# Attention with a routed FFN on one core: the first batch's second chunk takes its two reused pairs late, the FFN's weights load two chunks later, and the FFN stands back behind the routing

## The chip, the cores and the metric

One Trainium2 chip, of which the program uses one core. The metric is device microseconds for one execution, from the first to the last instruction with what lies around them; less is better.

## The reference

For each of 8 batches of 3136 tokens: attention without a softmax, whose output gates `u`, and then a small FFN for the 128 tokens of the batch that score highest.

```python
def _attn_ref(u, v, z):            # u, v: (8, 3136, 256)   z: (8, 3136, 64)
    scores = (1.0 / S) * np.matmul(z, z.transpose(0, 2, 1))
    attn = np.maximum(scores, 0.0) ** 2
    return u * np.matmul(attn, v)

def _moe_ref(x, w_gate, w1, w2, capacity):      # w1: (256, 1024)   w2: (1024, 256)   capacity 128
    scores = np.einsum('bsd,d->bs', x, w_gate)
    out = x.copy()
    for b in range(B):
        top_idx = np.argpartition(-scores[b], capacity)[:capacity]
        xe = x[b, top_idx]
        ye = np.maximum(xe @ w1, 0.0) @ w2
        g = 1.0 / (1.0 + np.exp(-scores[b, top_idx]))
        out[b, top_idx] = xe + g[:, None] * ye
    return out

reference = lambda u, v, z, ...: _moe_ref(_attn_ref(u, v, z), w_gate, w1, w2, capacity)
```

## The kernel before

**Chunks and slots.** Each batch is cut into 7 chunks of output tokens: five of 512 (called c0 to c4 here), then one of 256 (c5) and one of 320 (c6). Each chunk runs over the batch's 24 groups of 128 tokens in pairs, and over a last half group by itself, so a chunk has 13 slots, s0 to s12, and a batch 91. The slots of all batches stand in one list, `slots`, and one loop goes through it; its index is `k`, and `SLOTS` is 13. In a slot, `mix` issues the pair's 12 matmuls into the accumulators `acc` (8 with the high part `hi` of the squared scores, 4 with the low part `lo`; the half group has 4). While the slot runs, `more_scores` prepares the pair that is used three slots later.

**New and old pairs.** A new pair needs four matmuls `sc<-Z,ZH` and `sc<-Z,ZL`, and after them relu, square and the split into `hi` and `lo` on ScalarE, VectorE and GpSimd. The matrix of scores is symmetric. So the five chunks of 512 also transpose what later chunks need (tile `aT`, of which there are two), SyncE stores it to DRAM (`squares`, `squares_narrow`, `squares_own`), and the later chunk fetches it into `qk` (three buffers) instead of computing it: an old pair. An old pair costs TensorE 12 matmuls instead of 16. A fetch is issued seven slots ahead of its first use (`AHEAD`), or later if the three `qk` buffers are taken. In c1 the old pairs are (0, 1) and (2, 3); each chunk spreads its old pairs evenly among the new ones.

**What else stands in the slots.** `plan` is a table from a slot's number to functions: loads for the next batch, fetches, and for the first batch the FFN's weights. `weight_tasks` loads each of eight pieces of `w1` and `w2` through the staging tile `vst`, splits it on ScalarE and GpSimd into `w_here` (the two tiles `wh` and `wl`, 1 MB each) and `keep_weight` stores the split halves to DRAM (`w1h_there` and so on), since only one of the two matrices fits.

**The queue of small tasks.** When a batch's last slot has been issued, `route` puts a list of tasks in the queue `far`, and they are worked off during the next batch's slots, one at a time. A task is a list of matmuls to mix into a slot's own, then functions for the other engines, and, if it has a third entry, the number of slots until the next one may start (two without it). When a chunk ends, `finish` queues two tasks of its own, which go ahead of these at s2 and s5 of the next chunk. In order, a batch's routed part is:

- `fold`, then eight times `total`: a search for the 128th highest score, three slots apart;
- `ahead` (then `quotas` and `spans` on VectorE) and `take`, which find the chosen tokens;
- `bring_weight(1)`, by which SyncE loads the split `w1` into `wh` and `wl`, and `number`; `gather`; an empty task; `weigh`; `turn`;
- the FFN: `hidden` for the first 512 columns (6 matmuls of 512), `turn_h` (4 transposes), `hidden` for the others, `bring_weight(2)`, which puts `w2` in `wh` and `wl` in place of `w1`, `turn_h`, and last `back`: 24 matmuls of 256 columns into `y`, with `scatter` behind them.

In `back` the first four matmuls use `wh`, the fifth is the first that uses `wl`. Batches 0 to 4 (counted from 0) go through the whole list, each during the batch after it. Batches 5 and 6 (`put_off`) leave the FFN for the end, and the last batch has a scheme of its own.

**Queues.** Every engine takes its instructions in the order in which they were issued. SyncE issues nearly all transfers in one row, and each waits there until its buffer is free. `ps_m` is one PSUM bank that the small tasks use one after the other.

Of the kernel before, what the change touches and what calls it, by code (L numbers as in the profile page):

```python
# [85 lines left out]
def attention_then_routed_ffn(ctx: ExitStack, tc: tile.TileContext, zt, ut, v, wg, w1, w2, cst, cst16, keys, outs, at, cap):  # L86
# [16 lines left out]
    SLOTS = NJ // 2 + 1  # L103
# [75 lines left out]
    def keep_weight(i):  # L179
        for here, there in zip(w_here, w_there[i - 1]):  # L180
            nc.sync.dma_start(there.bitcast(F32), here.bitcast(F32))
# [126 lines left out]
    for b in range(B):  # L308
        for c in range(NCH):
            old = [(2 * g, 2 * g + 1) for g in range(min(c, WHOLE) * GT // 2)]  # L310
            new = [(2 * g, 2 * g + 1) for g in range(min(c, WHOLE) * GT // 2, NJ // 2)]
            if c < WHOLE and (b or c):

                new.insert(len(new) - 2, new.pop(1))
            both = [((i + 0.5) / len(old), 0, js, True) for i, js in enumerate(old)]
            both += [((i + 0.5) / len(new), 1, js, False) for i, js in enumerate(new)]
            slots += [(b, c, js, is_old) for _, _, js, is_old in sorted(both)]
            slots.append((b, c, (NJ,), False))
# [28 lines left out]
    def spend(act=0.0, dve=0.0, pool=0.0):  # L347
        busy["act"] += act
        busy["dve"] += dve
        busy["pool"] += pool  # L350
# [187 lines left out]
    def put_off(b):  # L538
        return B - 1 - HELD <= b < B - 1 and merged(B - 1) > 0

    def merged(b):
        return LATE if b == B - 1 and 0 < cap <= P else 0
# [121 lines left out]
    def route(b):  # L664
# [59 lines left out]
        def settle(rd):  # L724
            junk = moe.tile([TP, NS], F32, name="enough", tag="enough")[:R]
            m = moe.tile([TP, 1], F32, name="m", tag="m")[:R]
            nc.vector.tensor_scalar(
                junk, st["ps"][:R, :NS], float(cap), None, op0=ALU.is_ge, op1=ALU.add, accum_out=m
            )
            mi = moe.tile([TP, 1], I32, name="mi", tag="mi")[:R]  # L730
            nc.vector.tensor_copy(mi, m)
            base = moe.tile([TP, 1], I32, name="base", tag="base", bufs=2)[:R]
            if rd == last:
                base = st["ps"][:R, 64:65].bitcast(I32)
            if rd == 0:
                k = moe.tile([TP, 1], I32, name="place", tag="place")[:R]
                nc.vector.tensor_scalar(
                    k, mi, 32 - BITS, INT_MIN, op0=ALU.logical_shift_left, op1=ALU.bitwise_xor
                )
                flip = moe.tile([TP, 1], I32, name="flip", tag="flip")[:R]  # L740
                nc.vector.tensor_scalar(
                    flip, k, 31, 0x7FFFFFFF, op0=ALU.arith_shift_right, op1=ALU.bitwise_and
                )
                nc.vector.tensor_tensor(base, k, flip, op=ALU.bitwise_xor)
            else:
                nc.vector.tensor_scalar(
                    base, mi, 32 - BITS * (rd + 1), st["base"], op0=ALU.logical_shift_left, op1=ALU.bitwise_xor
                )
            st["base"] = base
            spend(dve=0.6)  # L750
# [69 lines left out]
        def spans(r0):  # L820

            rank = consts["rank"][:R, r0 : r0 + P]
            taken, begin, end = st["taken"], st["begin"], st["end"]
            if r0:
                nc.vector.tensor_scalar(taken[:, NT : NT + 1], begin, -float(r0), -2.0 * NT, op0=ALU.add, op1=ALU.max)
                nc.vector.tensor_scalar_min(taken[:, NT : NT + 1], taken[:, NT : NT + 1], 2.0 * P)
            else:
                nc.vector.tensor_scalar_min(taken[:, NT : NT + 1], begin, 2.0 * P)
            upper = moe.tile([TP, P], F32, name="upper", tag="upper")[:R]
            nc.vector.tensor_scalar(upper, rank, end, None, op0=ALU.is_le)  # L830
            of = moe.tile([TP, P], BF16, name="of", tag="big", bufs=2)[:R]
            nc.vector.scalar_tensor_tensor(of, rank, begin, upper, op0=ALU.is_gt, op1=ALU.mult)
            st["of"] = of
            spend(dve=0.6)
# [6 lines left out]
        tasks = [([fold], [start, count], 3)]  # L841
# [4 lines left out]
        if late:  # L846
            tasks.append(([total], [lambda: settle(last), masks]))
            tasks += [([columns], keep_columns), ([places], ranks)]
            tasks += choose(st, 0, cap)
            choice[b] = st  # L850
        else:
            tasks.append(([total], [lambda: settle(last), masks, run_up]))
            tasks.append(([ahead], [quotas, lambda: spans(0)]))
            for r0 in range(0, cap, P):
                n = min(P, cap - r0)
                first, *ffn = expert(b, st, n, r0)
                if put_off(b) and b == B - 2:
                    tasks = [(*t[:2], 2) for t in tasks]
                if r0:
                    tasks.append(([], lambda r0=r0: spans(r0)))  # L860
                tasks.append(([take], None))
                tasks += first
                if put_off(b):
                    held.append(ffn)
                else:
                    tasks += ffn[0] + ffn[1]
# [13 lines left out]
    def choose(st, r0, n):  # L880

        R, NT = st["G"].shape
        QT = Q // 4
        NP = NT // QT

        def pick(q):
            oh = moe.tile([TP, QT, P], BF16, name="oh", tag="big", bufs=2)[:R]
            t = slice(q * QT, (q + 1) * QT)
            nc.vector.tensor_tensor(
                oh,  # L890
                consts["rank"][:R, r0 : r0 + P].rearrange("p (o r) -> p o r", o=1).broadcast_to([R, QT, P]),
                st["rk"][:, t].rearrange("p (t o) -> p t o", o=1).broadcast_to([R, QT, P]),
                op=ALU.is_equal,
            )
            st["oh", q] = oh
            spend(dve=1.1)

        def find(q):
            if q == 0:
                st["ps"] = misc_bank("ids")  # L900
            what = st["what"]
            for i in range(QT):
                t = q * QT + i
                nc.tensor.matmul(
                    st["ps"][:, : what.shape[2]], st["oh", q][:, i, :], what[:, t, :],
                    start=(t == 0), stop=(t == NT - 1),
                )

        def begin():
            tok = consts["tok_half16"][:R].rearrange("p (t w) -> p t w", w=2)  # L910
            what = moe.tile([TP, NT, 5], BF16, name="what", tag="what")[:R]
            nc.vector.tensor_copy(what[:, :, :2], tok)
            cut(st["G"], what[:, :, 2:])
            st["what"] = what
            pick(0)

        tasks = [([], begin), ([], lambda: pick(1))]
        for q in range(NP):
            then = (lambda q=q: pick(q + 2)) if q + 2 < NP else None
            tasks.append(([lambda q=q: find(q)], then))  # L920
        tasks[-1] = (tasks[-1][0], lambda: keep_choice(st))
        return tasks
# [256 lines left out]
    def at_slot(k, fn, act=0.0, dve=0.0):  # L1179
        if k < len(slots):  # L1180
            plan.setdefault(max(k, 0), []).append((fn, act, dve))

    def at_slots(k, load, use, act, dve=0.0, lead=2):

        at_slot(k, use, act, dve)
        loads.append((k - lead, load))
# [3 lines left out]
    for b in range(B):  # L1190
        k0 = b * per

        for i in range(NCH):
            if b == 0:
                k = (0, 0, 0, 1, 3, 5, 6)[i]
            elif i < WHOLE:
                k = k0 - per + (i + 1) * SLOTS + 7
            else:
                k = k0 - 1 + 4 * (i - WHOLE)
# [9 lines left out]
        for g in range(NJ // 2 + 1):  # L1209
            k = k0 - 10 + 3 * g // 2 if b else max(1, g - 2)  # L1210
# [20 lines left out]
    for (b, c, g), ks in used.items():  # L1231
        k = max(ks[0] - AHEAD, room.popleft() - LEAD + 2)
# [4 lines left out]
            at_slot(k - LEAD - 3, lambda key=(b, c): fetch_own(*key))  # L1237

    for i, (load, use) in enumerate(weight_tasks):
        k = (1 + i // 4) * SLOTS  # L1240
        loads.append((k + (8, 9, 11, 13)[i % 4], load))
        at_slot(k + 10 + i % 4 * 2, use, 0.6)
    for i in (1, 2):
        at_slot(i * SLOTS + 17, lambda i=i: keep_weight(i))
    at_slots(SLOTS + 1, load_consts, use_consts, 0.0, 0.7)
    for k, load in loads:
        at_slot(k, load)
# [83 lines left out]
    for k, (b, c, js, is_old) in enumerate(slots):  # L1331
# [5 lines left out]
        tasks = []  # L1337
# [126 lines left out]
```

## Time and profile before

| | |
|---|---|
| runs | median 2114.52 us of 3 (2112.32, 2114.52, 2115.31) |
| profiled execution | 2112.72 us; span 2110.9 us from the first to the last instruction, so 1.8 us lie around it |
| granted TensorE clock | 1.00 throughout |
| busy share of the span | TensorE 99%, weight load 83%, VectorE 74%, GpSimd 62%, ScalarE 60% |
| DMA | 412 MB, 195 GB/s on average; SyncE's queue is busy 70% of 16 engines' span |

The busy share counts a matmul from its start to a modelled end, and consecutive ones overlap, so 99% does not say that TensorE runs at its best; it does say that little idle time is left. Rows of the timeline read: start, length, engine (with a q where it is the issue of a transfer), line, operation, tiles, shape, count, and in brackets the idle time before it and what ended that.

### The profile page before, as it was taken

Reading aid. Unit: us, or ns where it says so; the run is one execution under the profiler, and the core shown is the slowest. Engines: PE = TensorE matmul, PEld = TensorE weight load, DVE = VectorE, ACT = ScalarE, POOL = GpSimd, SP = SyncE. Lnnn points to the kernel's source line nnn. Section 1 sums busy time; section 2 is a strip of 40 time slices with the busy share of each in tenths; the row PEclk is TensorE's granted clock in tenths of the full one; section 3 lists DMA queues with packets and bytes.
Section 4 is the critical chain, followed back from the end, with each engine's and each line's share of the span. In section 5 each row is a group of like instructions: output and inputs, shape, how many; then the busy total and the mean of one; then the engine's idle time right before and its main releaser. Section 6 shows DMA issues by size and latency. Waiting matters only on the chain.

```text
span 2110.9 us, 31339 instructions
## 1 busy us (share of the span) xinstructions
PE 2081.4 (99%) x10359; PEld 1750.4 (83%) x10359; DVE 1559.2 (74%) x2361; ACT 1263.3 (60%) x1570; POOL 1313.5 (62%) x703
## 2 busy tenths in 40 slices
PE   8999999999999999999999999999999999999999
PEld 6788978889888898888888888888888888887788
DVE  8766678775877668776678767787577876788776
ACT  7665576554766457654576546765467654775543
POOL 6676577645766458664587646766467655666643
PEclk9999999999999999999999999999999999999999
DMA  6698766787668766688666876678766776666862
GB/s 189 202 261 222 198 184 173 217 199 213 181 186 218 202 195 190 188 220 220 177 190 187 229 211 173 190 195 217 210 182 185 196 193 171 203 188 162 220 173 96
DMA packets 425730, 412.01 MB, mean 195 GB/s; under 512 B 147616, under 2 KB 338912, under 8 KB 421984
## 3 DMA queue, kind: packets, MB, share of 16 engines
q1 hardware_dynamic: 424512, 407.66, 69.8%
q0 software_dynamic: 768, 2.10, 0.3%
q8 instruction: 81, 1.33, 0.3%
q14 instruction: 81, 0.66, 0.1%
q10 hardware_dynamic: 288, 0.26, 0.0%
HBM read 235.31 MB, written 172.23 MB: 193 GB/s over the span
## 4 chain that ended last, share of the span: by engine, by line
PE 74%; DVE 6%; DMA 6%; ACT 5%; POOL 3%; issue 3%; SPq 2%; POOLq 0%; ACTq 0%; DVEq 0%
PE acc L521 60%; PE sc L415 12%; DVE a L436 2%; POOL lo L485 2%; ACT a L425 2%; ACT hi L426 2%; DMA vst<-in_v 2%; DMA qk<-squares_narrow 1%; DVE aT L454 1%; DMA wl<-w2l_there 1%; DVE lo L485 1%; DMA squares_narrow<-aT 1%; PE h L1104 1%; PE y L1148 1%; SPq L265 0%
## 5 line engine op out<-in xcount | busy, mean ns | idle before, releaser
L521 PE MATMUL acc<-hi,V 128*128 128x512 f32 (+2 forms) x5376 | 1226.0, 366 | 9.0 <-ACT hi L393 4.7
L485 POOL TENSOR_TENSOR lo<-a,hi 128x1024 fp32r<-128x1024 f32 (+2 forms) x327 | 740.8, 2268 | 609.3 <-DVE a L436 438.9
L521 PEld LDWEIGHTS acc<-hi,V 128*128 128x128 f32 x5376 | 930.3, 188 | 175.9 <-DVE ut L566 9.1
L521 PE MATMUL acc<-lo,V 128*128 128x512 f32 (+2 forms) x2688 | 664.2, 364 | 7.2 <-POOL lo L485 3.5
L425 ACT ACTIVATE a<-sc 128x1024 f32<-128x1024 f32 (+4 forms) x408 | 363.2, 890 | 493.2 <-PE sc L415 374.9
L521 PEld LDWEIGHTS acc<-lo,V 128*128 128x128 f32 x2688 | 471.4, 188 | 89.0 <-DVE lo L485 6.4
L436 DVE TENSOR_TENSOR a<-sc,a 128x1024 f32<-128x1024 f32 (+3 forms) x335 | 339.9, 1015 | 258.1 <-ACT hi L426 227.9
L393 ACT CAST hi<-qk 128x1024 fp32r<-128x1024 f32 (+2 forms) x320 | 274.4, 862 | 254.5 <-PE acc L521 204.5
L485 DVE TENSOR_TENSOR lo<-qk,hi 128x1024 fp32r<-128x1024 f32 (+2 forms) x230 | 348.2, 1523 | 84.4 <-ACT hi L393 83.2
L454 DVE STREAM_TRANSPOSE aT<-a 128x512 f32<-128x512 f32 (+1 forms) x520 | 341.0, 691 | 89.5 <-ACT a L431 62.7
L426 ACT ACTIVATE hi<-a 128x1024 fp32r<-128x1024 f32 (+4 forms) x408 | 377.4, 925 | 21.4 <-PE acc L521 5.0
L415 PE MATMUL sc<-Z,ZH 128*128 128x512 f32 (+2 forms) x760 | 280.8, 373 | 3.7 <-DVE a L436 2.1
L415 PE MATMUL sc<-Z,ZL 128*128 128x512 f32 (+2 forms) x760 | 278.2, 370 | 0.7 <-DVE ZL L121 0.7
L485 POOL TENSOR_TENSOR lo<-qk,hi 128x512 fp32r<-128x512 f32 (+2 forms) x90 | 172.9, 1924 | 61.1 <-issue 45.5
L415 PEld LDWEIGHTS sc<-Z,ZH 128*128 128x128 f32 x760 | 142.6, 188 | 35.0 <-DVE a L436 7.7
L415 PEld LDWEIGHTS sc<-Z,ZL 128*128 128x128 f32 x760 | 142.6, 188 | 25.3 <-DVE ZL L121 1.1
L121 POOL TENSOR_TENSOR V<-vst,V 128x512 fp32r<-128x512 f32 x89 | 128.2, 1445 | 28.5 <-ACT V L120 22.4
L587 POOL TENSOR_TENSOR ut<-x,w_run 128x1024 f32<-128x1024 f32 (+2 forms) x52 | 124.3, 2390 | 26.5 <-DVE x L578 25.7
L121 POOL TENSOR_TENSOR ZL<-zst,ZH 128x512 fp32r<-128x512 f32 (+2 forms) x56 | 69.4, 1244 | 17.1 <-ACT ZH L120 17.1
L431 ACT ACTIVATE a<-a 128x1024 f32<-128x1024 f32 x73 | 77.5, 1062 | 2.3
L120 ACT CAST V<-vst 128x512 fp32r<-128x512 f32 x95 | 57.7, 608 | 30.0 <-DMA vst<-in_v 30.0
L566 DVE SCALAR_TENSOR_TENSOR ut<-acc,ut 128x512 f32<-128x512 f32 (+2 forms) x112 | 64.1, 613 | 12.6 <-PE acc L521 12.4
(173 smaller groups left out, 1054.6 us busy)
## 6 DMA issues: line engine op xcount, KB each, us to landing
squares<-aT SPq DMA_DIRECT2D x160, 512.0 KB
qk<-squares SPq DMA_DIRECT2D x320, 256.0 KB
squares_narrow<-aT SPq DMA_DIRECT2D x320, 128.0 KB
qk<-squares_narrow SPq DMA_DIRECT2D x80, 512.0 KB
vst<-in_v SPq DMA_DIRECT2D x190, 128.0 KB
out<-x SPq DMA_DIRECT2D x162, 128.0 KB
ut<-in_ut SPq DMA_DIRECT2D x40, 512.0 KB
squares_own<-aT SPq DMA_DIRECT2D x39, 256.0 KB
```

What stands on the lines that cost most here:

```text
L121: (lo_on or nc.vector.tensor_tensor)(lo, src, hi.bitcast(F32), op=ALU.subtract)
L393: nc.scalar.copy(by(hi), src)
L415: nc.tensor.matmul(ps[:, q], z[:, j * P : (j + 1) * P], mov, start=z is ZH, stop=z is ZL)
L425: nc.scalar.activation(a, ps[:, :n], AF.Relu)
L426: nc.scalar.activation(pieces[0][0](hi), pieces[0][1], AF.Square)
L431: nc.scalar.activation(a, a, AF.Square)
L436: square = lambda: nc.vector.tensor_tensor(a[rows], ps[rows, :n], a[rows], op=ALU.mult)
L454: nc.vector.transpose(to, a[rows, q].rearrange("p (m t a) -> p m t a", t=GT, a=Q))
L485: on.tensor_tensor(view(lo), src, view(hi).bitcast(F32), op=ALU.subtract)
L521: nc.tensor.matmul(ac[h], w, mov, start=first and h not in started, stop=stop)
L566: nc.vector.scalar_tensor_tensor(xT[:, h, :w], acc[b, c][h], SCALE * SCALE, xT[:, h, :w], op0=ALU.mult, op1=ALU.mult)
L587: nc.gpsimd.tensor_tensor(wx, runs, consts["wg_run"].rearrange("p (o r) -> p o r", o=1).broadcast_to([P, NB, RUN]), op=ALU.mult,)
```

## The change

Three edits, in the tables that place work in slots:

- In the first batch's second chunk (batch 0, c1) the two old pairs stand in the last 40% of the chunk instead of being spread evenly: at s7 and s10 instead of s2 and s8.
- The weights' eight loads, their splits and the two `keep_weight` stores stand two chunks (26 slots) later.
- `ahead` is followed by three slots of rest instead of two, and `take` by thirteen instead of two (two as before where the FFN is put off). So `take` moves from s10 to s11 of c2, and all that follows it in batches 1 to 5 moves by about 11 slots: `bring_weight(1)` from s0 to s11 of c3, the first `hidden` from s0 to s10 of c4, `bring_weight(2)` from s8 of c4 to s6 of c5, the second `turn_h` from s10 of c4 to s8 of c5, and `back` from s0 to s10 of c5.

```diff
-            both = [((i + 0.5) / len(old), 0, js, True) for i, js in enumerate(old)]
+            wait = 0.6 if (b, c) == (0, 1) else 0.0
+            both = [(wait + (1 - wait) * (i + 0.5) / len(old), 0, js, True) for i, js in enumerate(old)]
...
-            tasks.append(([ahead], [quotas, lambda: spans(0)]))
+            tasks.append(([ahead], [quotas, lambda: spans(0)], 3))
...
-                tasks.append(([take], None))
+                tasks.append(([take], None, 2 if put_off(b) else 13))
...
     for i, (load, use) in enumerate(weight_tasks):
-        k = (1 + i // 4) * SLOTS
+        k = (3 + i // 4) * SLOTS
...
-        at_slot(i * SLOTS + 17, lambda i=i: keep_weight(i))
+        at_slot((i + 2) * SLOTS + 17, lambda i=i: keep_weight(i))
```

SyncE's row around `bring_weight(2)` in batch 1, before. `qk` with a number is a buffer that a fetch fills, `squares_narrow1_2` is what chunk 2 stored for c5 and c6; these rows stand at the end of c4.

```order
L468 DMA squares_narrow1_4_111<-aT_4464 32x4x256 x4
L185 DMA wh_82<-w2h_there_88 128x2048
L185 DMA wl_83<-w2l_there_89 128x2048
L468 DMA squares_narrow1_4_111<-aT_4514 32x4x128 x2
L369 DMA qk_4543<-squares_narrow1_2_107 128x2x512
L369 DMA qk_4572<-squares_narrow1_3_109 128x2x512
```

The same row after the change, in c5 (lines below the first edit are one higher): `out_1<-x` stores c4's output, `Z_4682` is filled for c6, and `qk_4689` is c6's first fetch.

```order
L586 DMA out_1<-x_4536 32x16x64 x4
L265 DMA Z_4682<-ZH_90 64x4x32 x2
L267 DMA Z_4682<-ZH_90 64x64
L265 DMA Z_4682<-ZL_91 64x4x32 x2
L267 DMA Z_4682<-ZL_91 64x64
L370 DMA qk_4689<-squares_narrow1_0_103 128x2x512
L373 DMA qk_4689<-squares_narrow1_0_103 128x256
L185 DMA wh_82<-w2h_there_88 128x2048
L185 DMA wl_83<-w2l_there_89 128x2048
L557 DMA ut_4718<-in_ut 128x2x256
```

The load stood behind a store of c4's last columns; it now stands behind c4's output, six transfers that fill `Z`, and c6's first fetch.

TensorE's row at the start of `back` in batch 1, before: the last slot of c4 (`Vr`), then the first of c5 with the first matmuls into `y`.

```order
L521 MATMUL acc_4243<-hi_4505,Vr_2907 128x512 x2
L521 MATMUL acc_4244<-hi_4505,Vr_2907 128x512 x2
L521 MATMUL acc_4574<-hi_4524,V_2368 128x256 x3
L1148 MATMUL y_4579<-wh_82,hh_4357 128x256 x2
L521 MATMUL acc_4574<-hi_4524,V_2368 128x256
L1148 MATMUL y_4579<-wh_82,hh_4357 128x256 x2
L521 MATMUL acc_4574<-lo_4541,V_2368 128x256
L1148 MATMUL y_4579<-wl_83,hh_4357 128x256 x3
```

After, in s8 to s10 of c5: the second group of transposes `hT`, one new pair (s9), and then `back`.

```order
L1121 MATMUL hT_4755<-c_sb_634,hr_4645 128x128 x4
L522 MATMUL acc_4545<-hi_4706,V_2841 128x256 x4
L522 MATMUL acc_4546<-hi_4706,V_2841 128x256 x4
L416 MATMUL sc_4774<-Z_4376,ZH_90 128x256
L416 MATMUL sc_4774<-Z_4376,ZL_91 128x256
L522 MATMUL acc_4545<-lo_4716,V_2841 128x256
L522 MATMUL acc_4546<-lo_4716,V_2841 128x256
L522 MATMUL acc_4545<-lo_4716,V_2841 128x256
L522 MATMUL acc_4546<-lo_4716,V_2841 128x256
L522 MATMUL acc_4545<-hi_4730,V_2695 128x256 x3
L1149 MATMUL y_4790<-wh_82,hh_4573 128x256 x2
```

`back` still starts two tasks behind `bring_weight(2)`, four slots later, but these four are slots of 256 columns instead of 512.

SyncE's row at the end of batch 0's first chunk, before, where `qk_513` is the fetch for c1's two old pairs:

```order
L556 DMA ut_477<-in_ut 128x2x512
L460 DMA squares0_0_92<-aT_469 512x1x256
L279 DMA vst_510<-in_v 64x256 x2
L364 DMA qk_513<-squares0_0_92 32x4x512 x4
L468 DMA squares_narrow0_0_93<-aT_502 32x4x256 x4
```

And after:

```order
L279 DMA vst_510<-in_v 64x256 x2
L469 DMA squares_narrow0_0_93<-aT_502 32x4x256 x4
L469 DMA squares_narrow0_0_93<-aT_539 32x4x256 x4
L469 DMA squares_narrow0_0_93<-aT_572 32x4x128 x2
L476 DMA squares_own0_1_113<-aT_601 128x512
L129 DMA c_sb_634<-in_cst 128x547
L131 DMA k_sb_636<-in_keys 98x120
L134 DMA w_bc_638<-in_wg 128x256
L138 DMA w_run_640<-in_wg 32x64 x4
L144 DMA zst_645<-in_cst16 128x388
L461 DMA squares0_1_94<-aT_629 512x1x256
L365 DMA qk_671<-squares0_0_92 32x4x512 x4
```

The fetch has moved from ahead of the ten `squares_narrow` stores to behind them, the constants' loads and the first store of c1.

## The prediction

> **What bounds the kernel now.** I read the page's first lines, then TensorE's waits, then the timelines of SyncE and TensorE at the places where the moved work stood and where it will stand.
>
> ```profile
> span 2110.9 us, 31339 instructions
> PE 2081.4 (99%) x10359; PEld 1750.4 (83%) x10359; DVE 1559.2 (74%) x2361; ACT 1263.3 (60%) x1570; POOL 1313.5 (62%) x703
> ```
>
> TensorE is the bound, and the change neither adds nor removes a matmul. So the time can change only by TensorE's stops: those of now that go, and those that are new. The list of its waits (total us, times, longest) shows what can go:
>
> ```profile
> PE acc L521 <- ACT hi L393: 4.7, 5, 1.7
> PE acc L521 <- POOL lo L485: 3.5, 3, 2.4
> PE y L1148 <- DMA wl<-w2l_there: 1.6, 3, 0.8
> PE taken L838 <- DVE of L832: 1.1, 6, 0.2
> ```
>
> A stop costs somewhat more than its idle time, because the pipeline drains and refills. The longest shows it:
>
> ```profile
> 59.77 1.07 PE L521 MATMUL acc<-hi,V 128*128 128x512 f32 x4
> 63.26 0.74 PE L521 MATMUL acc<-lo,V 128*128 128x512 f32 x2 [2.42 <-POOL lo L485]
> 63.83 0.40 PE L415 MATMUL sc<-Z,ZH 128*128 128x512 f32 x1
> 64.07 0.40 PE L415 MATMUL sc<-Z,ZL 128*128 128x512 f32 x1
> 16.40 1.98 PE L521 MATMUL acc<-hi,V 128*128 128x512 f32 x8
> ```
>
> In the last row eight matmuls take 1.98 us and one 0.39, so starts are (1.98 - 0.39) / 7 = 0.227 us apart. Four from 59.77 make the next due at 60.68; it came at 63.26, 2.58 late, with 2.42 idle. The two from 63.26 took 0.57 until the next instead of 0.45. I count 0.25 us beside the idle time of each stop.
>
> **The moved FFN: the load of `w2` against `back`.** This is the large term. In the present place:
>
> ```profile
> 473.72 0.39 SPq L185 DMA_DIRECT2D wh<-w2h_there  x1
> 480.52 0.51 PE L521 MATMUL acc<-hi,V 128*128 128x256 f32 x3
> 482.19 0.62 PE L1148 MATMUL y<-wl,hh 128*128 128x256 f32 x3 [0.45 <-DMA wl<-w2l_there]
> 993.79 0.39 SPq L185 DMA_DIRECT2D wh<-w2h_there  x1
> 1000.61 0.52 PE L521 MATMUL acc<-hi,V 128*128 128x256 f32 x3
> 1001.74 0.62 PE L1148 MATMUL y<-wl,hh 128*128 128x256 f32 x3
> 1514.68 0.40 SPq L185 DMA_DIRECT2D wh<-w2h_there  x1
> 1523.50 0.50 PE L1148 MATMUL y<-wl,hh 128*128 128x256 f32 x2 [0.78 <-DMA wl<-w2l_there]
> ```
>
> The first use of `wl` came 8.47 us after the issue of the `wh` load in batch 1, 8.82 in batch 5, both released by the transfer; in batch 3, 7.95 us was enough. I take 8.3 us. Unhindered, that use is due 1001.74 - 1000.61 = 1.13 us into the slot. In c4 there are about 6.8 us between issue and slot (480.52 - 473.72), so the wait is short. In c5 it is not. The place where the load will stand can be read in batch 0, which has no FFN in its c5:
>
> ```profile
> 222.00 0.64 PE L521 MATMUL acc<-hi,V 128*128 128x256 f32 x4
> 228.66 2.83 SPq L585 DMA_DIRECT2D out<-x  x4
> 231.59 1.77 SPq L265 DMA_DIRECT2D Z<-ZH  x2
> 236.13 0.52 SPq L369 DMA_DIRECT2D qk<-squares_narrow  x1
> 237.26 0.38 SPq L556 DMA_DIRECT2D ut<-in_ut  x1
> 237.56 0.64 PE L521 MATMUL acc<-hi,V 128*128 128x256 f32 x4
> 476.43 0.60 PE L1120 MATMUL hT<-c_sb,hr 128*128 128x128 f32 x4
> 476.79 2.08 PE L521 MATMUL acc<-hi,V 128*128 128x512 f32 x8
> ```
>
> c5 begins at 222.00, its s10 at 237.56, 15.56 us later. With the FFN there, s0 to s9 also hold two groups of transposes (476.43 to 476.79, 0.36 us each) and six matmuls of 512 columns (6 x 0.227 = 1.4), so s10 begins at 15.56 + 0.7 + 1.4 = 17.7 and the first use of `wl` is due at 18.8. SyncE: `out<-x` went out 6.7 us into the chunk, then `Z`, then c6's first fetch, and the row between that and `ut`, where the load will stand, is at 237.2, 15.2 us in. The stores wait for VectorE, which now starts some tenths later (a transpose group on TensorE and `hl` ahead of it), so 15.7. Then the use can begin at 15.7 + 8.3 = 24.0 instead of 18.8: TensorE stops for 5.2 us, part of it before the first `wh` matmul, part before the first `wl`; with the refill 5.3. Five batches: +26.5 us. Nothing covers it, because every matmul of the slot stands in the same row. It is shorter only if SyncE gets through its row sooner (0.8 us less if `Z`'s transfers wait for nothing) or the bytes arrive sooner, and longer if they arrive later:
>
> ```profile
> 475.00:482.00 7.00, 6.74 (x36) 5.55 (x35) 3.89 (x6) 2.45 (x4) 1.83 (x2) 1.00 1.00 365
> 1017.00:1027.00 10.00, 8.28 (x62) 7.55 (x61) 4.92 (x8) 3.74 (x7) 3.74 (x3) 1.00 0.70 233
> ```
>
> While the load runs in c4, the DMA engines are busy all the time at 365 GB/s (last two columns); around c6's first fetches they moved 233 GB/s at 0.70. The fetch, issued 1.1 us ahead of the load, adds 0.64 MB to its 2.1. At 365 GB/s the 2.7 MB need 7.5 us, at 233 GB/s 11.8: 6.4 to 10.7 us from the load's issue, and a stop of 3.3 to 7.6 us. 8.3 us lies between them, nearest to what this load itself has shown. [...]
>
> What the same move takes away: the present wait for `wl` (1.6 idle, 3 stops: 2.3 us). And c6's start:
>
> ```profile
> 1024.35 0.41 PE L521 MATMUL acc<-hi,V 128*128 128x320 f32 x1 [1.66 <-ACT hi L393]
> 1284.43 0.56 PE L521 MATMUL acc<-hi,V 128*128 128x320 f32 x2 [1.08 <-ACT hi L393]
> 1545.75 0.56 PE L521 MATMUL acc<-hi,V 128*128 128x320 f32 x2 [1.30 <-ACT hi L393]
> 763.29 1.35 ACT L393 CAST hi<-qk 128x640 fp32r<-128x640 f32 x2 [2.26 <-DMA qk<-squares_narrow]
> ```
>
> There ScalarE waits for c6's first fetch. That fetch will go out some 14 us into its chunk, as in batch 0 (236.13), ahead of the load, and TensorE will reach c6 some 6 us later than now: all three stops go, 4.0 + 3 x 0.25 = 4.8 us. Late next is `lo` for c6's first pair: VectorE makes it with the second of two instructions behind `back`, while TensorE still has s11, s12 and four matmuls of c6 to do; I take it as covered.
>
> `bring_weight(1)` at the end of c3 is needed twelve slots later, 36 us: hidden. Its 2.1 MB ahead of c4's fetches and of the stores that free `aT` delay these by up to 8 us; a fetch is wanted four slots (12 us) after its issue there. 0, at most 1 us a batch.
>
> **The longer rest before `take`.** Six times TensorE waited for `of` at s10; a slot later it is there: 1.1 + 6 x 0.15 = 2.0 us gained. No other task uses the PSUM bank in the 13 slots.
>
> **The first batch's old pairs.** The 2.42 us stop at 63.26 was GpSimd's, which had waited 6.08 us for VectorE, which had waited for a store:
>
> ```profile
> 49.65 2.00 SPq L364 DMA_DIRECT2D qk<-squares  x4
> 51.75 8.57 SPq L468 DMA_DIRECT2D squares_narrow<-aT  x10
> 58.80 0.71 DVE L454 STREAM_TRANSPOSE aT<-a 64x512 f32<-64x512 f32 x1 [3.19 <-DMA squares_narrow<-aT]
> 60.84 4.72 POOL L485 TENSOR_TENSOR lo<-a,hi 128x1024 fp32r<-128x1024 f32 x2 [6.08 <-DVE a L436]
> ```
>
> The stores stood behind the fetch; now they don't, and the 2.0 us of issue and 1 MB are gone from ahead of them. VectorE's 3.19 us shrink by 2 us or all. I take 2.5 of the 2.7 us of the stop. The fetch, put behind the first store of c1, can delay the stores after it by the same 2 us: bounds 0 and 2.7, nearer the upper one, as c1 had no other long stop.
>
> **The weights two chunks later.** c1 and c2 lose, c3 to c5 gain the same splits and 4.2 MB of stores. In c5 the last store goes ahead of c6's first fetch, whose ScalarE copy TensorE already waits for in batch 0 (one of the five `hi` waits). In its present place:
>
> ```profile
> 164.06 0.64 SPq L181 DMA_DIRECT2D w2h_there<-wh  x1
> 165.98 0.34 SPq L181 DMA_DIRECT2D w2l_there<-wl  x1
> ```
>
> it takes 2.3 us of SyncE's row. Once: 0 to 3 us, I take 0.8.
>
> **Sum.** 26.5 - 2.3 - 4.8 - 2.0 - 2.5 + 0.8 = +15.7 us: span 2110.9 + 15.7 = 2126.6. The profiled execution was 2112.72 us, 1.8 over its span, and lies 1.8 under the median of the runs, so I say 2129.
>
> **Rivals.**
>
> (a) The load is hidden, and only the gains stay. It would have to be issued 18.8 - 8.3 = 10.5 us into c5, ahead of `Z`; the issue row speaks against it, and that ten 1.5 us slots are short. Then -2.3 - 4.8 - 2.0 - 2.5 + 0.8 = -10.8: 2104. Chance 0.08.
>
> (b) The load comes about half as late, since SyncE's row clears early and the emptier c5 lets the bytes through. A stop of 2.7 us: 5 x 2.6 = 13 less, 2116. The DMA share of 0.70 in this stretch speaks for it, the 0.64 MB just ahead against. 0.14.
>
> (c) Bytes arrive at the slower rate: 7.6 us a stop, 5 x 2.3 = 11 more, 2140. 0.2.
>
> (d) TensorE restarts slowly after these stops. At the start of the program it does:
>
> ```profile
> 1.20 4.11 PE L1295 MATMUL idle<-zero 128*128 128x512 bf16 x12 [1.20 <-DVE zero L1292]
> ```
>
> Twelve matmuls took 4.11 us where 12 x 0.227 + 0.16 = 2.9 would do, 1.2 us more. Five times that, 6 us: 2135. Against it: after the 2.42 us stop the starts are 0.24 apart at once (63.83, 64.07), and the new stop is in two parts of 2 to 3 us. [...] 0.08.
>
> (e) c3 to c5 of the first batch, or c4 of the others, cannot take what is moved there: 5 us more, 2134. 0.05.
>
> **How the numbers follow.** The forecast has 0.45, at 2129 (2123 to 2135 by its own bounds). What a measurement can tell from no change is 0.2%, 4.2 us. (a) is faster: 0.08. (b) straddles the upper edge of 2118.7: 0.09 of it within, the rest slower. All else is slower: 0.83. The range leaves out (a) and the ends of (b) and (c): 2116 to 2141.
>
> **What would show it.** In the waits, `y` for `wh<-w2h_there` or `wl<-w2l_there` ten times, 20 to 30 us together; the load's issue 15 to 16 us after c5's first matmul; `hi` waits of L393 near 0.4; no wait for `of`; no 2.42 us stop at c1's start. c5 of batch 3, now 23.7 us (1000.61 to 1024.35), should last about 6 us longer: the stop and the 2.1 us that moved in, less the stops that go. If `y` waits for nothing, the forecast is wrong at its first step.

## The result, and the profile after

| | before | after |
|---|---|---|
| median of 4 runs each | 2114.63 us | 2142.19 us |
| lowest to highest | 2112.32 to 2115.31 | 2138.54 to 2142.91 |
| ratio, 95% interval | | 1.0133 [1.0118, 1.0147] |
| profiled execution (span) | 2112.72 (2110.9) | 2138.54 (2136.8) |
| mean granted TensorE clock | 1.00 | 0.992 |

The change costs 27.6 us, 1.3%. The forecast, 2129 (2116 to 2141), had the sign right, was 13 us too low, and the time lies 1.2 us above its range.

The head of the page of after, and the longest of TensorE's waits (total us, times, longest us):

```profile
span 2136.8 us, 31360 instructions
PE 2090.0 (98%) x10359; PEld 1762.2 (82%) x10359; DVE 1533.8 (72%) x2354; ACT 1268.1 (59%) x1572; POOL 1326.9 (62%) x708
```

```profile
PE y L1149 <- DMA wh<-w2h_there: 14.2, 5, 3.6
PE y L1149 <- DMA wl<-w2l_there: 6.0, 5, 1.5
...
PE acc L522 <- ACT hi L394: 3.7, 2, 2.3
```

The same number of matmuls, and `y` waits ten times for the load of `w2`, 20.2 us together, where it waited 1.6 us before. The two waits for `hi` are both in the first batch, and the wait of `taken` for `of` is no longer in the list. SyncE's row in c5 of batch 1, which begins at 482.2:

```profile
488.54 2.27 SPq L586 DMA_DIRECT2D out<-x  x4
490.90 2.79 SPq L265 DMA_DIRECT2D Z<-ZH  x2
...
496.43 0.53 SPq L370 DMA_DIRECT2D qk<-squares_narrow  x1
497.56 0.38 SPq L185 DMA_DIRECT2D wh<-w2h_there  x1
```

The load goes out 15.3 us into the chunk. TensorE at `back` in the same batch, and in batch 3:

```profile
500.03 0.52 PE L522 MATMUL acc<-hi,V 128*128 128x256 f32 x3
503.38 0.76 PE L1149 MATMUL y<-wh,hh 128*128 128x256 f32 x2 [2.83 <-DMA wh<-w2h_there]
...
1032.71 0.48 PE L1149 MATMUL y<-wh,hh 128*128 128x256 f32 x2 [2.28 <-DMA wh<-w2h_there]
1033.03 0.28 PE L522 MATMUL acc<-hi,V 128*128 128x256 f32 x1
1033.15 0.40 PE L1149 MATMUL y<-wh,hh 128*128 128x256 f32 x2
...
1035.14 0.94 PE L1149 MATMUL y<-wl,hh 128*128 128x256 f32 x3 [1.48 <-DMA wl<-w2l_there]
...
1036.10 0.41 PE L1149 MATMUL y<-wl,hh 128*128 128x256 f32 x1
1036.31 0.41 PE L1149 MATMUL y<-wh,hh 128*128 128x256 f32 x1
```

The stop in two parts stands as forecast. The last rows are the second loss: a matmul of 256 columns takes 0.41 us where it took 0.28, and starts are 0.21 apart (1036.10 to 1036.31) where 0.12 is usual (1033.03 to 1033.15). The granted clock explains it. Stretches of after, first five of about 3.4 us just ahead of the fall of the clock (762.00 and 765.50 follow on each other), then two of the six at half clock. Columns: length, busy time of PE, PEld, DVE, ACT and POOL, then the granted clock, DMA share and GB/s.

```profile
499.30:502.70 3.40, 1.25 (x11) 1.04 (x9) 1.42 (x3) 0.80 (x2) 1.86 (x2) 1.00 1.05 425
762.00:765.50 3.50, 3.15 (x27) 2.95 (x26) 2.29 (x3) 2.01 (x4) 3.50 (x3) 1.00 0.97 287
765.50:768.90 3.40, 0.66 (x5) 0.69 (x6) 0.64 (x2) 0.00 (x0) 0.28 (x1) 1.00 0.99 402
1294.60:1298.00 3.40, 0.07 (x1) 0.10 (x1) 0.67 (x2) 0.00 (x0) 0.32 (x1) 1.00 0.98 405
243.40:246.80 3.40, 1.22 (x11) 1.01 (x9) 0.00 (x0) 0.66 (x2) 0.00 (x0) 0.99 0.90 270
...
246.70:250.20 3.50, 3.29 (x12) 3.29 (x13) 2.32 (x4) 0.79 (x2) 0.00 (x0) 0.51 1.01 354
502.70:509.60 6.90, 5.42 (x24) 5.16 (x25) 0.00 (x0) 0.73 (x1) 0.00 (x0) 0.51 0.98 372
```

Where TensorE was busy only 0.07 to 1.25 us of 3.4, the clock then falls to half for 3.4 or 6.8 us; after 762.00 to 765.50, with 3.15 us, it does not. There are six half-clock stretches, some 31 us together: one in the first batch, and one at `back` in each of batches 1 to 5.

To place all of the loss I took the starts of TensorE's matmuls in each profiled execution and summed by place what lies beyond the usual distance (0.228, 0.145 and 0.117 us for 512, 320 and 256 columns). In us:

| | before | after | difference | forecast |
|---|---|---|---|---|
| stops before `y`, batches 1 to 5 | 2.1 | 22.2 | +20.0 | 26.5 - 2.3 = +24.2 |
| matmuls at half clock | 0 | 12.4 | +12.4 | 0 |
| c6 of batches 1 to 5 | 17.3 | 8.7 | -8.6 | -4.8 |
| stop before `taken` | 2.1 | 0.0 | -2.1 | -2.0 |
| first batch, c1 | 3.1 | 1.8 | -1.3 | -2.5 |
| first batch, c5 and c6 | 4.2 | 8.5 | +4.3 | +0.8 |
| all else | 42.1 | 42.7 | +0.6 | 0 |
| sum | 70.9 | 96.3 | +25.4 | +15.7 |

The spans differ by 25.9. This table, made in the same way of each experiment, is what is called the loss below.

### The profile page after: what moved, and what is told of

Same layout as the page of the kernel before. It is cut to its first block, busy times and chain, and to the rows that moved or that the text cites. A ratio compares the mean times of both kernels' runs of the same rounds, so it can differ in the third digit from the quotient of the medians.

```text
span 2136.8 us, 31360 instructions
## 1 busy us (share of the span) xinstructions
PE 2090.0 (98%) x10359; PEld 1762.2 (82%) x10359; DVE 1533.8 (72%) x2354; ACT 1268.1 (59%) x1572; POOL 1326.9 (62%) x708
## 4 chain that ended last, share of the span: by engine, by line
PE 81%; DMA 5%; DVE 3%; ACT 3%; issue 3%; SPq 2%; POOL 2%; POOLq 0%; DVEq 0%; ACTq 0%
PE acc L522 66%; PE sc L416 12%; DMA wl<-w2l_there 2%; POOL lo L486 1%; ACT a L426 1%; ACT hi L427 1%; DVE a L437 1%; PE y L1149 1%; DMA vst<-in_w 1%; PE h L1105 1%; DMA squares<-aT 1%; DVE lo L486 1%; SPq L265 1%; DMA vst<-in_v 1%; DVE aT L455 0%
## 5 line engine op out<-in xcount | busy, mean ns | idle before, releaser
L486 DVE TENSOR_TENSOR lo<-qk,hi 128x1024 fp32r<-128x1024 f32 (+2 forms) x226 | 332.6, 1479 | 86.0 <-ACT hi L394 74.0
L486 POOL TENSOR_TENSOR lo<-qk,hi 128x1024 fp32r<-128x1024 f32 (+2 forms) x94 | 180.8, 1926 | 42.4 <-ACT hi L394 33.3
L121 POOL TENSOR_TENSOR ZL<-zst,ZH 128x512 fp32r<-128x512 f32 (+2 forms) x56 | 71.3, 1279 | 21.9 <-ACT ZH L120 17.1
L120 ACT CAST V<-vst 128x512 fp32r<-128x512 f32 x95 | 57.9, 609 | 25.4 <-DMA vst<-in_v 25.2
```

The lines of the kernel that those rows point to most:

```text
L121: (lo_on or nc.vector.tensor_tensor)(lo, src, hi.bitcast(F32), op=ALU.subtract)
L486: on.tensor_tensor(view(lo), src, view(hi).bitcast(F32), op=ALU.subtract)
```

## The experiments

Each was timed beside runs of the kernel before on the same chip; the ratio is to those. The theory to test was that the late load costs twice, once as the stop before `y` and once as half clock after it, and that the first batch's weights cost more than forecast. The rivals were that the load's bytes or the moved FFN cost in themselves, and that another edit carries the loss.

**e1: after, with the rest behind `take` as before.**

```diff
-                tasks.append(([take], None, 2 if put_off(b) else 13))
+                tasks.append(([take], None))
```

> The changed kernel with take's rest back at two slots, so that the FFN stands where it stood before; the other edits stay. Theory A (the cost is the load of w2 that back waits for in c5, 20 us, and the half clock after it, about 11 us in batches 1 to 5): both go, c6's stops of before return, what is left is -2 for take, -1.3 at the first batch's c1 and about +6 in its c5 and c6: 2115 to 2120, and the clock is at half speed once at most. Theory B (the first batch's edits or the moved weights carry the cost): above 2130.

Measured: 2119.88 us, 1.0023 [1.0008, 1.0038]. The stops before `y` fall to 3.2 and the half clock to 1.6, all of it in the first batch. So this one edit carries some 22 us of the change, as the theory had it. It remains slower than before, by what the first batch loses (6.7 in c5 and 4.5 in c6).

**e2: before, with both rests alone.**

> The kernel before with the two rests alone (three slots behind ahead, thirteen behind take). Theory A: 2114.6 + 20 (y's stops) + 11 (half clock) - 2 (take) - 9 (c6's stops go) = 2135, 2132 to 2138. Theory B: 2120 or less.

Measured: 2138.49 us, 1.0123 [1.0092, 1.0153]; stops before `y` 23.0, half clock 11.1 in five places, c6 of batches 1 to 5 at 10.1, no stop before `taken`. The time is half a microsecond past the 2132 to 2138 that was expected. The rests alone bring both losses, and the gain at c6.

**e3: after, with the load of `w2` issued earlier**, with the second `hidden`'s work; the FFN stays where it is. On SyncE it then stands right behind `out<-x`, ahead of `Z`.

```diff
-        return first, [], [hid[0], tur[0], hid[1], ([], lambda: bring_weight(2)), tur[1], (to_y, scatter)]
+        hid[1] = (hid[1][0], [hid[1][1], lambda: bring_weight(2)])
+        return first, [], [hid[0], tur[0], hid[1], ([], None), tur[1], (to_y, scatter)]
```

> The changed kernel with the load of w2 issued right behind the second hidden (s3 of c5) and an empty task in its old place, so that back stays at s10. On SyncE it then stands ahead of Z and of c6's first fetch. Theory A (the load is merely issued too late): it goes out about 9 us into c5, 8.3 us later is 17.5, back needs it at 18.8; y's stops (22 us) and the half clock (11) of batches 1 to 5 go: 2109 to 2117. Theory C (c5's transfers leave no room for 2 MB wherever it is issued): the wait moves to c6's first slot, 3 us or more a batch, 2125 or more.

Measured: 2109.73 us, 0.9984 [0.9970, 0.9997]: by the ratios 31 us less than after, with the same bytes and the same FFN in the same slots. SyncE and TensorE of e3 in batch 1:

```profile
492.53 2.23 SPq L586 DMA_DIRECT2D out<-x  x4
494.87 1.21 SPq L185 DMA_DIRECT2D wh<-w2h_there  x1
```

```profile
504.39 0.40 PE L1149 MATMUL y<-wh,hh 128*128 128x256 f32 x2
...
505.45 0.62 PE L1149 MATMUL y<-wl,hh 128*128 128x256 f32 x3 [0.19 <-DMA wl<-w2l_there]
```

The `wh` matmuls wait for nothing and the first with `wl` for 0.19 us. Stops before `y` are 1.8 in all, and no half clock is left in batches 1 to 5. So the late issue, not the bytes and not the place of the FFN, is the cause of both. In the first batch three half-clock stretches stood (4.7 us).

**e4 and e8: after, with needless matmuls ahead of the first `y` of batches 1 to 5**, 20 in e4 and 40 in e8. They add work and keep TensorE busy while the load is awaited; their results are overwritten.

```diff
+                for _ in range(40 if not roomy else 0):
+                    nc.tensor.matmul(st["ps"][:, :D], consts["c16"][:, :P], consts["c16"][:, :D], start=True, stop=True)
```

> The changed kernel with 20 matmuls of 256 columns on constants ahead of back's first, into y's bank, which back's first matmul overwrites: 2.3 us of TensorE work in a stop of 2.5 to 3.8 us. Theory D (a 3.4 us window in which TensorE is busy for less than about 0.3 halves the clock for the next one, and this costs 10 to 11 us in batches 1 to 5): the stop stays as long but counts as busy, the clock stays full in batches 1 to 5, 2130 to 2134. Theory E (the slow matmuls are the waits' own, and the clock record costs nothing): 2142, or up to 2150 if the dummies push back out.

> The kernel after with 40 needless matmuls of 256 columns ahead of the first y of each of batches 1 to 5 (20 in e4). They cost 40 x 0.117 = 4.7 us in each batch, 23.4 in all, and take the place of stops of 2.8 and 1.2 us. If half clock follows from how little TensorE did in the 3.41 us before (theory D), no half-clock window is left in batches 1 to 5: 2142 + 23.4 - 20 - 10.8 = 2134, at most 2137. If half clock comes with the late load itself, whatever TensorE does meanwhile, some 10 us of it stay and the time is 2143 to 2147.

Measured: e4 2138.46 us, 1.0115 [1.0087, 1.0143]; e8 2137.46 us, 1.0102 [1.0087, 1.0116]. In e4 the stops fall to 14.1 and the half clock in batches 1 to 5 from 10.8 to 5.6: 20 were too few, stops of 2 to 3.5 us remained, and 2130 to 2134 was missed. Its four runs took 2140.6, 2140.5, 2136.5 and 2134.5 us at mean clocks of 0.995, 0.995, 0.997 and 0.999. In e8 the half clock in batches 1 to 5 is 1.6, and the stops 5.0. Added work of 23.4 us made nothing slower. By the table: stops -17.1, half clock in batches 1 to 5 -9.3, added +23.4, the first batch's c5 and c6 +2.6, other places +0.5; 0.1 in all, as the spans show (2136.8 and 2136.9). The time is half a microsecond past the end of what was expected of half clock. Only one stop is left after which the clock falls, TensorE in batch 2 of e8:

```profile
765.81 3.66 PE L1148 MATMUL y<-c 128*128 128x256 bf16 x32
769.55 0.51 PE L1152 MATMUL y<-wh,hh 128*128 128x256 f32 x2
...
773.35 0.62 PE L1152 MATMUL y<-wl,hh 128*128 128x256 f32 x3 [2.81 <-DMA wl<-w2l_there]
...
774.51 0.84 PE L1152 MATMUL y<-wh,hh 128*128 128x256 f32 x3
```

The load goes out equally late in all five batches, 14.4 to 14.9 us into c5. Where the needless matmuls fill the stop the clock stays; where 2.81 us remain, the next matmuls are 0.21 apart again (three in 0.84). So the half clock follows from TensorE's stop and not from the load.

**e5 and e12: before, with the first batch's weights later alone**, two chunks in e5 (the change's own edit), one in e12.

```diff
-        k = (1 + i // 4) * SLOTS
+        k = (3 + i // 4) * SLOTS
...
-        at_slot(i * SLOTS + 17, lambda i=i: keep_weight(i))
+        at_slot((i + 2) * SLOTS + 17, lambda i=i: keep_weight(i))
```

> The kernel before with the first batch's weights and their stores two chunks later, nothing else. If the forecast's term was right (+0.8), 2114 to 2116. If the term was too small and what the first batch's chunks 5 and 6 lost in the kernel after (+4.3 of stops and up to 1.7 of half clock) belongs to the weights, 2118 to 2121. If those stops came from another part of the change, 2114 and the first batch's chunk 5 stays at its 0.4 of stops.

> The kernel before with the first batch's weights and their stores one chunk later in place of two: the second weight's parts are then loaded and split in chunk 4, whose matmuls stand 39 us, and not beside the narrow work of chunk 5 with its 19 to 25 us. If e5's 10.6 come from chunk 5 (SyncE's queue, ScalarE's casts and GpSimd's subtractions have no room there), this is within 2 of before: 2113 to 2116, with 0.4 of stops in the first batch's chunk 5. If any later place costs, in proportion, 2117 to 2120.

Measured: e5 2125.32 us, 1.0041 [1.0028, 1.0054]; e12 2121.09 us, 1.0025 [1.0014, 1.0035]. Both are slower, e5 by more than even the larger value expected. The loss of e5 against before: first batch's c5 +4.8 and c6 +1.2, half clock +3.3 in two stretches, both in the first batch. TensorE, ScalarE and SyncE of e5 where c5 begins:

```profile
225.21 0.74 PE L521 MATMUL acc<-hi,V 128*128 128x256 f32 x4 [2.65 <-ACT hi L393]
...
227.10 0.42 PE L415 MATMUL sc<-Z,ZH 128*128 128x256 f32 x1
```

```profile
224.01 0.62 ACT L120 CAST wh<-vst 128x512 fp32r<-128x512 f32 x1 [7.46 <-DMA vst<-in_w]
224.54 1.13 ACT L393 CAST hi<-qk 128x512 fp32r<-128x512 f32 x2
```

```profile
205.87 3.58 SPq L585 DMA_DIRECT2D out<-x  x4
209.55 0.50 SPq L181 DMA_DIRECT2D w1h_there<-wh  x1
...
210.63 2.54 SPq L265 DMA_DIRECT2D Z<-ZH  x2
...
217.34 0.46 SPq L175 DMA_DIRECT2D vst<-in_w  x1
```

The load of a piece of `w2` leaves SyncE at 217.34, behind the stores and `Z`. ScalarE takes its row in order: from 216.55 it stands 7.46 us before the piece's cast, and the cast `hi<-qk` that TensorE needs stands behind it. TensorE stops for 2.65 us and goes on at half clock (0.42 a matmul). Before, it stood 2.87 us at most for a piece, in c2. The same stretch of both kernels, before first, then e5:

```profile
222.00:250.00 28.00, 27.35 (x210) 26.35 (x209) 17.20 (x22) 13.41 (x22) 15.24 (x10) 1.00 0.72 198
```

```profile
222.00:250.00 28.00, 21.76 (x161) 20.72 (x159) 13.43 (x14) 11.93 (x22) 19.31 (x13) 0.94 0.83 262
```

210 matmuls lie in it before, 161 in e5. The forecast costed only the last store here. e12 shows that it is not c5's narrow slots alone: with the weights in c3 and c4 the first batch's c4 loses 5.3 (0.3 before), and half clock follows at 189.6. TensorE and ScalarE of e12:

```profile
188.91 1.52 PE L521 MATMUL acc<-hi,V 128*128 128x512 f32 x4 [2.35 <-ACT hi L393]
```

```profile
187.29 0.62 ACT L120 CAST wh<-vst 128x512 fp32r<-128x512 f32 x1 [7.53 <-DMA vst<-in_w]
```

It is the same chain, with 7.53 us. So the reading that only c5 has no room for the weights is refuted.

**e9: e5 with the first two pieces of `w2` loaded five slots earlier.**

```diff
-        loads.append((k + (8, 9, 11, 13)[i % 4], load))
+        loads.append((k + (8, 9, 11, 13)[i % 4] - (5 if i in (4, 5) else 0), load))
```

> e5 (the weights two chunks later alone, 2125.3) with the loads of the first two parts of the second weight five slots earlier (slots 3 and 4 of chunk 5's count in place of 8 and 9); the casts and everything else stay. If e5's loss comes from ScalarE standing 7.46 us before wh<-vst with hi<-qk behind it, chunk 5's 4.8 of stops fall to about 1 and the half-clock window behind them (1.6) goes: 2125.3 - 3.8 - 1.6 = 2120, 2118 to 2122; the stop at the start of chunk 6 (2.7) stays. If e5's loss comes from the bytes or from the casts' own time on ScalarE and GpSimd, 2124 to 2126.

Measured: 2122.77 us, 1.0046 [1.0033, 1.0059]. By the ratio that is no gain over e5's 1.0041, and c5's loss is still 4.0: what was expected did not come. The time lies between what the two readings gave. ScalarE and TensorE of e9 show why:

```profile
228.16 0.62 ACT L120 CAST wh<-vst 128x512 fp32r<-128x512 f32 x1 [2.30 <-DMA vst<-in_w]
231.93 0.62 ACT L120 CAST wh<-vst 128x512 fp32r<-128x512 f32 x1 [2.11 <-DMA vst<-in_w]
```

```profile
237.83 0.74 PE L521 MATMUL acc<-lo,V 128*128 128x256 f32 x4 [1.12 <-POOL lo L485]
248.55 0.85 PE L521 MATMUL acc<-hi,V 128*128 128x320 f32 x4 [3.50 <-ACT hi L393]
```

The first piece is cast at 216.44, ScalarE does not wait for it, and the loss in c5's first slot is gone: c5 begins at 222.4 us, against 225.2 in e5 and 222.0 before. So the chain is as it was read, and of e5's two half-clock stretches (3.3 us of loss) one is gone with it (1.6 left). But c5 now loses 3.6 in s4 to s7, where ScalarE waits for the two pieces that were not moved and GpSimd's `lo` is late, and the stop at the start of c6 is 3.50 us instead of e5's 2.73, since c6's first fetch goes out 21 us into c5 (14 before). So the weights cost there in more than one place; the shares of SyncE's row, the bytes and the casts are not told apart. This profiled execution took 2117.8 us and was the shortest of the five, so it need not show all that the median lost.

**e6: before, with the two old pairs late alone.**

> The kernel before with the two old pairs of the first batch's second chunk late, nothing else. By the forecast's term (-2.5) 2112; by what the kernel after showed there (-1.25, since a new stop of 1.6 us comes at slot 6) 2113.3; a rival in which the pairs only move the stop gives 2114.5.

Measured: 2111.50 us, 0.9985 [0.9975, 0.9994], by the medians 3.2 us less, as much as the forecast's term. But the trace does not show that gain in c1. The 2.42 us stop is gone, and another stands at s6:

```profile
64.27 2.50 SPq L365 DMA_DIRECT2D qk<-squares  x4
66.86 2.87 SPq L461 DMA_DIRECT2D squares<-aT  x2
74.84 1.30 DVE L455 STREAM_TRANSPOSE aT<-a 128x512 f32<-128x512 f32 x2 [3.73 <-DMA squares<-aT]
77.99 2.43 POOL L486 TENSOR_TENSOR lo<-a,hi 128x1024 fp32r<-128x1024 f32 x1 [4.61 <-DVE a L437]
86.16 1.21 PE L522 MATMUL acc<-lo,V 128*128 128x512 f32 x4 [1.89 <-POOL lo L486]
```

It is the chain of before, at another place: stores behind the fetch in SyncE's row, VectorE waiting for a store, GpSimd for VectorE, TensorE for GpSimd. The loss of c1 falls from 3.1 to 2.3, that of c2 rises from 0.2 to 0.7, and c3 begins at 145.8 us instead of 146.0. So in this execution the pairs moved the stop and gained next to nothing; e7's is the same there (c3 at 145.9). This execution, at 2113.5 us, is the fourth longest of twelve and has a half-clock stretch in batch 3's c6. Where the rest of the 3.2 us comes from is not shown.

**e10: before, with the rest behind `take` and e3's early load.**

> The kernel before with the rest of 13 behind `take` alone and the load of the second weight issued early as in e3; no rest behind `ahead`, no change in the first batch. If the rest behind `take` is what shortens the starts of chunk 6 (some 8 us over five batches) and the stop before `taken` (2.0), 2104.5 to 2107. If the rest behind `ahead` carries that, only the 2.0 goes: 2112 to 2113.

Measured: 2106.18 us, 0.9967 [0.9954, 0.9980]. c6 of batches 1 to 5 falls from 17.3 to 8.0, so the rest behind `take` carries that gain (e1, without it, has 16.0). The stop before `taken` stays, 2.1 as before; it goes only with the third slot of rest behind `ahead` (e2, e7). So the time lies in the expected range, though one of its two terms did not come.

**e11: after, with both early loads (e3's and e9's).**

> The kernel after, whole, with both repairs: the second weight of batches 1 to 5 issued as in e3, and the first batch's second weight loaded as in e9. From e3's 2109.7 the first batch's chunk 5 gives back 3.8 and one half-clock window 1.6: 2104 to 2106. If e9's repair does nothing, 2109 to 2111.

Measured: 2107.25 us, 0.9969 [0.9957, 0.9981]; 2104.18 to 2114.14 in nine runs. That is past the end of the 2104 to 2106 that the repair was to give. It is below e3's 2109.73, another chip's number, but the intervals of the ratios overlap. The profiled execution was the longest of the nine and is of little use here.

**e7: both rests, e3's early load and the pairs late, the weights as before.**

> The kernel before with both rests, the load of the second weight issued with the second hidden layer's work as in e3, and the pairs late; the first batch's weights stay where they are before the change. If the first batch's extra stops and half clock come from its weights, e3's 2109.7 falls by the 4.3 of stops and by up to 3.3 of half clock: 2102 to 2106. If they come from the pairs or from elsewhere, 2109 to 2110.

Measured: 2103.57 us, 0.9946 [0.9933, 0.9960], 11.2 us faster than before. It differs from e3 in the weights alone: 0.9984 against 0.9946, 0.38% or 8 us, which agrees with e5. The loss: stops before `y` 2.0, half clock 0, first batch's c5 0.4, c6 of batches 1 to 5 8.3, none before `taken`. Its span, 2101.3 us, is 9.6 us under that of before, as the losses are (61.0 against 70.9).

## Why the prediction fell short

**The stop before `y`: right, a little too large.** The issue came 15.3, 14.5, 14.4, 14.9 and 14.8 us into c5, forecast 15.7. The first use of `wl` came 8.2 to 9.5 us after it, 8.7 on average, forecast 8.3. So it stood 23.5 us in, forecast 24.0, and the stop with its refill was 22.2 / 5 = 4.4 us instead of 5.3. e3 shows that it is the issue that decides, as the prediction had it. Rival (a) described what e3 does: issue ahead of `Z` hid the load there, with 1.8 us of stops before `y` left in all. Rival (c), slower bytes, gave 2140, the nearest of all to the 2142 measured, but by luck: at its rate the first use would have come 10.7 us after the issue, not 8.7.

**Half clock: the step that failed.** The main forecast had none. Rival (d) had it at five times 1.2 us, 6 us, with a chance of 0.08; the runs show 10.8 in those five places and 1.6 in the first batch, 12.4. The 1.2 was read off the program's start, where starts are 0.43 us apart for only 2.9 us and then 0.21; behind these stops the half clock lasted 3.4 or 6.8 us. The arguments against it were that after the 2.42 us stop of before the next starts are 0.24 apart at once, and that the new stop is in two parts of 2 to 3 us. The second took the length of one gap for the measure: in after the two parts at `back` of batch 3, 2.28 and 1.48 us, left 1.00 us of work in 3.5 (1031.70 to 1035.20), and half clock followed. The first was one case: in e12, which does not touch it, the same stop was followed by half clock:

```profile
63.54 1.22 PE L521 MATMUL acc<-lo,V 128*128 128x512 f32 x2 [2.50 <-POOL lo L485]
64.56 0.63 PE L415 MATMUL sc<-Z,ZH 128*128 128x512 f32 x1
64.98 0.63 PE L415 MATMUL sc<-Z,ZL 128*128 128x512 f32 x1
```

Starts are 0.42 apart here and 0.24 in the rows that the prediction shows. The forecast fell short by 13 us. The profiled execution lay 10 above its sum for it (2126.6 + 1.8 = 2128.4): in these 10, half clock is 12.4 and the first batch 4.7 (c5, c6 and c1 against their terms), less 8.0 at `y` and c6. The median lay another 3.7 above that execution, which was the fastest of the four; what the others lost was not traced. For the median the prediction's own steps give 2130.2 (the 1.8 by which the profiled execution lies under the median is named, but not added), not 2129.

**The first batch's weights: the term that was mis-sized.** +0.8 with bounds of 0 to 3; after lost 4.3 in c5 and c6 and 1.6 at half clock, and e5 alone is 8.7 us slower by its ratio. The prediction priced the store in SyncE's row and let the splits weigh the same wherever they stand. What it missed is the cast of a piece that is not there yet, in ScalarE's row ahead of `hi<-qk`: the load goes out later in SyncE's row than in c1 and c2, and the row of ScalarE does not move with it. e9 shows that this cast is not all: with it repaired, other pieces' casts, GpSimd's work and c6's late fetch still cost as much. The sign that the prediction named, `hi` waits near 0.4, came out at 3.7, both of them in the first batch's c5 and c6. Rival (e) held that c3 to c5 cannot take it, +5 us, at a chance of 0.05.

**c6's start: right, too small.** -4.8, measured -8.6. The list of waits gave three stops; the starts show a loss of 0.9 to 2.5 us in the first slot of c6 in all five batches before, 8.6 together, and 0.1 after. TensorE, before, in batch 1, and after, in batch 3:

```profile
503.15 0.84 PE L521 MATMUL acc<-hi,V 128*128 128x320 f32 x4
504.01 0.56 PE L521 MATMUL acc<-lo,V 128*128 128x320 f32 x2
```

```profile
1041.88 0.75 PE L522 MATMUL acc<-hi,V 128*128 128x320 f32 x4
1042.47 0.46 PE L522 MATMUL acc<-lo,V 128*128 128x320 f32 x2
```

No bracket stands in the rows of before, and yet from the first `hi` on 320 columns to the first `lo` are 0.86 us instead of 0.59. Waits shorter than what the list reports add up. Of the two reasons given, an earlier fetch and a later TensorE, the first is enough: in e7, where TensorE hardly stops before `y`, c6's first fetch goes out 15.2 to 16.5 us into c5 (17.1 to 18.9 before), and the loss in c6 is 8.3 all the same.

**`taken`: right.** -2.1 for -2.0; the edit is the rest behind `ahead`, though the prediction headed it as the one before `take`.

**The old pairs: the stop went, the gain did not follow as reckoned.** The term took 2.5 of 2.7 us and named as its lower bound that the fetch may delay the stores behind it. It does: in after a new stop of 1.5 us at c1's s6 leaves a gain of 1.3, and in e6 and e7, with 1.8 to 1.9 us there, hardly anything is left by the start of c3. That e6's median fell by 3.2 does not bear out this mechanism.

c5 of batch 3 lasted 29.7 us, 6.0 more than before, as forecast. That agreement hid two errors: a loss before `y` of 4.1 where 5.3 was said, and 1.6 of half clock.

## What to carry to other kernels

When work is moved past a chunk's border, follow each transfer it issues through its queue to the place where its result is used, and each instruction that waits for it through its engine's row to what stands behind: here ScalarE stood 7.5 us before a cast of 0.6 us, and TensorE stopped for 2.65 us behind it. Price TensorE's stops with the half clock that may follow them (here 33 us for 20 of idle time; one stop of 2.3 us was enough in after's first batch), and repair the issue before giving up the move: with the load in front, the longer rest gained 7 us (e10), where with the late load both rests cost 25 (e2). And time the parts of a bundle alone, and read the trace of each: here the weights lost 9, the rests lost only for want of an earlier issue, and the pairs' 3 us are not where they were looked for.

## What the hardware showed that was not expected

In after half clock came on a fixed beat. The six stretches begin at 246.8, 502.8, 769.0, 1035.2, 1298.1 and 1564.3 us, all within 2 ns of multiples of 3.4133 us from each other, and each lasts one or two beats (3.413 or 6.827 us). Counting a matmul as busy for the usual distance given above for its columns, and without the program's first 8 and last 5 us, all six beats of after at full clock and up to 0.31 busy were followed by half clock, and none of its others at full clock, which begin at 0.40; before has no beat under 0.42 and no half clock. Over the profiled executions with such a stretch it was all 30 cases up to 0.38 busy, one of three between 0.38 and 0.41, and none from 0.42 on. In after's first batch a stop of 2.3 us lay almost wholly within one beat (243.4 to 246.8, 0.31 busy), and half clock followed. In before the 2.42 us stop that ends at 63.26 lay across two (from 58.6 and from 62.0, 0.60 and 0.53 busy, if its beat is the one on which its clock falls at 2110.0), and none followed. At this place, c1's start, half clock followed in e12 and not in before, e2, e5 and e9. e4's four runs spread over 6 us along with their clock, 0.995 to 0.999. The length of a single gap did not decide: half clock followed gaps of 1.7 us (e6, at 1024) to 3.6 us (after), while in before none followed the 2.42 us.

A transfer that was issued sooner took longer: e3's load, issued at 494.87, served the first `wl` at 505.45, 10.6 us later, while in after the same bytes took 8.2 us from 497.56; `Z`'s transfers now went out right behind it, but that they are the cause was not tried.
